# A retention-attention kernel with two feed-forward layers: fewer filler matmuls at the first pair, and two rows of weights converted later in the attention

## The chip, the cores and the metric

The kernel runs on one core of one Trainium2 chip. The metric is device time in microseconds (us), the median of repeated executions. Three executions of the kernel before took 845.58, 846.1 and 847.55 us, so its median is 846.1 us.

## The reference

The program computes a retention attention (no softmax: the scores are multiplied by a decay table), and then two feed-forward layers on its output. Cut to what matters:

```python
scores = q @ k.T / sqrt(64)                  # 4 batches, 8 heads, 576 positions, 64 wide
ret    = (scores * Dmat) @ v                 # Dmat[n, m] = gamma_h ** (n - m) for n >= m, else 0
x  = ret as (2304 tokens, 512)
h  = x @ w_in                                # layer one: 512 -> 2048 -> 512
x  = (max(h, 0) + alpha * min(h, 0)) @ w_out
h  = x @ w2_in                               # layer two, the same sizes
out = (h / (1 + exp(-1.702 * h))) @ w2_out
```

The weights of both layers arrive as 64-bit floats. The kernel turns them into 32-bit floats on the chip, and each of those into two words, high and low, whose three largest cross products stand for one product.

## The kernel before, in words

**Attention.** The 32 heads are worked in 16 pairs. Pair i loads its `ld` (queries, keys, values, 864 KB) and `kts` (keys once more, 256 KB). TensorE computes the scores (`sc`, `a_scores`), then the states (`st`, `a_outer`), and after them the values of the pair before (`av`, `a_values`). VectorE multiplies the scores by the decay (`r`, L305), sums the states (L320, L325, L330) and takes the finished values of the pair before out of PSUM (`xs`, L350). ScalarE scales `kts` and takes the states out. So in pair i VectorE does r(i), the three sums of i, and xs(i-1), in that order, and TensorE's `av` of pair i waits for xs(i-1), which frees its PSUM bank. At pair 0 there is no pair before; `fill(14)` puts 14 matmuls on zeros there (`wps`, L708), and 8 more stand at the very start.

**Weight rows.** Layer one's weights come in 16 rows (128 of the 2048 hidden channels each; 128 x 1024 64-bit numbers in two loads, `raw`). A row is converted by one ScalarE operation (`w_abs`, L116), and on VectorE by two tensor_scalar operations (`w_clamp`, L120 and L123), `w_top` (L130) and `w_low` (L137). Then ScalarE copies the high words (`w_hi`, L85) and VectorE subtracts to get the low words (`w_lo`, L88). `raw` has two slots, so the load of row m waits for `w_low` of row m-2. Between these, `xa_split` cuts finished attention output into high and low words for layer one.

**Order.** Every engine works in program order. The order of the row operations is written as a list of events with due times: `at(t, ...)` puts one in, and `run_to(t)`, called at fixed places of the pair loop (at i, i + 0.25 and i + 0.75), emits all that are due. One unit of time is one pair; layer one starts at `base` = 17 and one unit there is one step. `pace` has the due time of each row, `ahead` how much earlier its load is issued, `d` the distance of its operations.

**Layer one.** A step multiplies one block of tokens by one row: `mm1` (12 matmuls of 512 columns into `h`, L403), then the activation (two ScalarE operations L413, L414 and one VectorE operation L415 into `g`), its split into two words (`gsf`, ScalarE L85 and VectorE L88), and `mm2` (12 matmuls into `acc`, L446), which comes two steps later. So TensorE's order at the start is mm1 of steps 0, 1 and 2 (36 matmuls), mm2 of step 0, mm1 of step 3, and so on. Steps 0, 1 and 2 use rows 0, 1 and 2. The first two matmuls of a step's mm1 need only the high words of its row, the third is the first that needs the low words.

Of the kernel before, what the change touches and what calls it, by code (L numbers as in the profile page):

```python
# [39 lines left out]
def kernel(  # L40
# [52 lines left out]
    def at(time, fn, *args):  # L93
        events.append((time, len(events), fn, args))

    def run_to(time):
        while events and events[0][0] <= time:
            _, _, fn, args = events.pop(0)
            fn(*args)
# [46 lines left out]
    def w_lo(key):  # L146
        sub(nc.vector, wt[key][:, 1], cvs.pop(key).rearrange(both, c=2), wt[key][:, 0])

    def w_words(t, key, src, ahead, d):
        at(t - ahead, w_load, key, src, key[1] % 2)  # L150
        at(t - ahead + (1.0 if ahead > 2 else 0), w_piece, key, src, 1)
        for i, fn in enumerate((w_abs, w_clamp, w_top, w_low)):
            at(t + d * i, fn, key)

    def quarter(j, e, c):
        return cvs[2, 2 * j + e][:, c * 256:c * 256 + 256]
# [80 lines left out]
    def a_load(i):  # L237
        b, p = PAIRS[i]
        t = tmp("ld", i, [128, 1728])
        if i == 0:  # L240
            nc.sync.dma_start(out=t[:, 0:512], in_=qkv[b, p, :, 0:512])
            nc.sync.dma_start(out=mask_sb, in_=mask)
            nc.sync.dma_start(out=vtab_sb, in_=vtab)
            nc.sync.dma_start(out=t[:, 512:1152], in_=qkv[b, p, :, 512:1152])
            nc.sync.dma_start(out=kts[:, 0], in_=kn[b, p])
            nc.sync.dma_start(out=t[:, 1152:1728], in_=qkv[b, p, :, 1152:1728])
        else:
            nc.sync.dma_start(out=t, in_=qkv[b, p])
            nc.sync.dma_start(out=kts[:, i % 4], in_=kn[b, p])
        if i == 1:  # L250
            nc.sync.dma_start(out=otab_sb[:, :, 0:128], in_=otab)
        q = [t[:, j * 128:j * 128 + 128] for j in (0, 1, 4, 5)] + [t[:, 768:832]]
        k = [t[:, j:j + 128] for j in (256, 384, 832, 960)] + [t[:, 1088:1152]]
        ld[i] = q, k, t[:, 1152:1728].rearrange("p (n d) -> p n d", n=9)
# [4 lines left out]
    def a_tables(p):  # L259
        for e in range(2):  # L260
            scale(diag_sb[:, p, e, 0], mask_sb[:, 0:128], vtab_sb[:, p, e:e + 1])
        scale(tail_sb[:, p], mask_sb[:, 128:192], vtab_sb[:, p, 2:3])

    def a_otab(p):
        o = otab_sb[:, p]
        for n in (128, 256):
            copy(o[:, n:2 * n], o[:, 0:n])
        copy(o[:, 512:S], o[:, 0:S - 512])
# [6 lines left out]
    def a_keys(i):  # L275
        n = kts[:, i % 4].rearrange("p (j n) -> p j n", j=4)
        for e, o in enumerate(halves):
            scale(n[:, :, o], n[:, :, o], vtab_sb[:, PAIRS[i][1], e:e + 1])
        k_t[i] = n

    def a_scores(i):
        q, k = ld[i][0:2]
        t = aps.tile([128, 2, 512], F32, tag="sc", name="sc", bufs=2)
        for j in range(4):
            for e, o in enumerate(halves):
                mm(t[:, e, j * 128:j * 128 + 128], k[j][o], q[j][o], j == 0, True)
        sc_t[i] = t

    def a_outer(i):
        q, k, v = ld[i]  # L290
        t = s_t[i] = aps.tile([128, 512], F32, tag="st", name="st")
        for o in halves:
            mm(t[o, 0:64], k[4][o], q[4][o], True, True)
        n = k_t.pop(i)
        for j in range(4):
            for e, o in enumerate(halves):
                mm(t[o, j * 64 + 64:j * 64 + 128], n[:, j, o], v[:, 2 * j + e], False, True)

    def a_evac(i):
        r = tmp("r", i, [128, 1600])  # L300
        r_t[i] = (
            r[:, 0:1024].rearrange("p (e n) -> p e n", e=2), r[:, 1024:1536],
            r[:, 1088:1600].rearrange("p (b n) -> p b n", b=2)[:, :, 0:64],
        )
        nc.vector.tensor_tensor(  # L305
            out=r[:, 0:1024].rearrange("p (e j n) -> p e j n", e=2, j=4),
            in0=sc_t.pop(i).rearrange("p e (j n) -> p e j n", j=4),
            in1=diag_sb[:, PAIRS[i][1]].to_broadcast([128, 2, 4, 128]), op=ALU.mult,
        )


    def a_states(i):
        p = PAIRS[i][1]
        s = r_t[i][1]
        scale(s[:, 0:320], s_t.pop(i)[:, 0:320], vtab_sb[:, p, 3:4])

    def a_sums(i):
        p = PAIRS[i][1]
        s = r_t[i][1]
        nc.vector.scalar_tensor_tensor(  # L320
            out=s[:, 320:512], in0=s[:, 64:256], scalar=vtab_sb[:, p, 3:4], in1=s[:, 128:320],
            op0=ALU.mult, op1=ALU.add,
        )
        half = r_t[i][2]
        nc.vector.scalar_tensor_tensor(  # L325
            out=s[:, 384:512].rearrange("p (b n) -> p b n", b=2), in0=half,
            scalar=vtab_sb[:, p, 4:5], in1=s[:, 384:512].rearrange("p (b n) -> p b n", b=2),
            op0=ALU.mult, op1=ALU.add,
        )
        nc.vector.tensor_tensor(out=s[:, 0:64], in0=s[:, 0:64], in1=tail_sb[:, p], op=ALU.mult)  # L330

    def a_values(i):
        q, _, v = ld[i]
        r, s = r_t.pop(i)[0:2]
        t = av_t[i] = aps.tile([128, 1024], F32, tag="av", name="av")
        out = [t[:, A0 + j * 128:A0 + j * 128 + 128] for j in range(4)] + [t[:, A0 + 512:A0 + S]]
        for c in range(1, 5):
            s0 = 64 if c == 1 else 192 + c * 64
            for o in halves:
                mm(out[c][o], s[o, s0:s0 + 64], q[c][o], c < 3, False)  # L340
        for o in halves:
            mm(out[4][o], v[o, 8], s[o, 0:64], False, True)
        for j in range(4):
            for e, o in enumerate(halves):
                mm(out[j][o], v[:, 2 * j + e], r[:, e, j * 128:j * 128 + 128], False, True)

    def a_out(i):
        if i % 3 == 0:
            xs_t[i // 3] = tmp("xs", i // 3, [128, 3, S])
        nc.vector.tensor_tensor(  # L350
            out=xs_t[i // 3][:, i % 3], in0=av_t.pop(i)[:, A0:A0 + S], in1=otab_sb[:, PAIRS[i][1]],
            op=ALU.mult,
        )
        ld.pop(i)
# [326 lines left out]
    wz = att.tile([128, 128], F32, name="wz")  # L681
    n_a = len(PAIRS)
    base = n_a + 1
    pace = [3.6, 8.6, 14.1]
    pace += [base + t for t in (0.8, 2.35, 3.9, 5.45, 7.0, 8.8, 10.6, 12.4, 14.2, 15.9, 17.6, 19.3, 21.4)]
    ahead = {0: 2.6, 1: 3.2, 2: 3.2}
    for m, t in enumerate(pace):
        d = 0.75 if m < 3 else 0.5
        w_words(t, (1, m), w1, ahead.get(m, 1.6), d)
        at(t + 3 * d + 0.25, w_hi, (1, m))  # L690
        at(t + 4 * d + 0.25, w_lo, (1, m))
    for i in range(n_a):
        b = PAIRS[i][0]
        for c in range(2):
# [6 lines left out]
    with tc.manual_schedule():  # L701
# [4 lines left out]
        def fill(n):  # L706
            for i in range(n):
                nc.tensor.matmul(out=wps[:, 0, 0:128], lhsT=wz, rhs=wz, start=True, stop=True)  # L708
# [5 lines left out]
        for i in range(n_a + 1):  # L714
            if i < n_a:
                a_scores(i)
                if i < NP:
                    a_tables(i)
                a_keys(i)
                a_evac(i)  # L720
            run_to(i)
            if i < n_a:
                a_outer(i)
                a_states(i)
                a_sums(i)
            run_to(i + 0.25)
            if i:
                if i <= NP:
                    a_otab(i - 1)
                a_values(i - 1)  # L730
                a_out(i - 1)
            else:
                fill(14)
            if i + 3 < n_a:
                a_load(i + 3)
            run_to(i + 0.75)
# [14 lines left out]
        for n, (_, c, m0, _) in enumerate(BLOCKS[N_FIRST:], 1):  # L751
            homes[c] = xp[n % 2]
            for k in range(NK):
                t = starts[c, m0] - (4 if n == 1 else 4.4) + 0.9 * k
# [160 lines left out]
```

## Time and profile before

| | |
|---|---|
| median of three executions | 846.1 us |
| the profiled execution | 845.46 us, its span 843.7 us, mean granted TensorE clock 0.993 |
| TensorE matmuls | busy 826.7 us, 98% of the span |
| TensorE weight loads | 753.0 us, 89% |
| VectorE | 633.7 us, 75% |
| ScalarE | 458.5 us, 54% |
| attention, from the first instruction to layer one's first matmul | 80.27 us |

The profile is one execution, in microseconds from its first instruction. A row of the timeline gives the start, the time until the last of its merged instructions ended, the engine (PE is TensorE, PEld its weight loads, DVE VectorE, ACT ScalarE), the source line, the operation with out<-in, and in brackets how long the engine had stood idle before it and what ended that. On TensorE one 32-bit matmul of the attention is recorded as two.

### The profile page before, as it was taken

The numbers are of one execution on the slowest core, as the hardware profiler recorded it, in microseconds if no ns is written. First come the engines' busy times: TensorE is split into PE (matmuls) and PEld (weight loads), VectorE is DVE, ScalarE is ACT, GpSimd is POOL, SyncE is SP. The second block draws the span as 40 slices with busy tenths as digits, with TensorE's granted clock in tenths as the row PEclk, the third lists the DMA queues.
The fourth block names the chain that finished last, engine by engine and source line by source line (L and its number), as shares of the span: only waits on it lengthen the run. The fifth ranks groups of instructions, "written<-read, shape, count | busy, mean of one in ns | idle before, by whom it ended". The sixth has DMA issues, their size and how long they took to land.

```text
span 843.7 us, 13989 instructions
## 1 busy us (share of the span) xinstructions
PE 826.7 (98%) x5132; PEld 753.0 (89%) x5132; DVE 633.7 (75%) x1128; ACT 458.5 (54%) x920; POOL 17.7 (2%) x36
## 2 busy tenths in 40 slices
PE   9999999999999998899999999999999999999998
PEld 8788888888888886698888899999999999999998
DVE  3997887687483776666768697789787699677875
ACT  5643664554353445445534676666566576566553
POOL 0000000000000010000010000000000000000000
PEclk9999999999999999999999999999999999999999
DMA  8985843455065465646656544598543877545872
GB/s 309 318 302 171 271 154 104 151 188 175 18 234 204 115 201 172 204 154 205 194 151 219 198 157 132 197 325 303 179 130 109 319 265 269 172 130 177 293 271 78
DMA packets 66100, 166.97 MB, mean 198 GB/s; under 512 B 7152, under 2 KB 33392, under 8 KB 60272
## 3 DMA queue, kind: packets, MB, share of 16 engines
q1 hardware_dynamic: 61424, 149.30, 51.8%
q0 software_dynamic: 4608, 16.78, 6.8%
q8 instruction: 40, 0.66, 0.3%
q14 instruction: 28, 0.23, 0.1%
HBM read 128.83 MB, written 37.22 MB: 197 GB/s over the span
## 4 chain that ended last, share of the span: by engine, by line
PE 55%; DMA 3%; DVE 2%; issue 1%; ACT 1%; SPq 0%; DVEq 0%; ACTq 0%
PE acc L567 23%; PE h L567 18%; PE acc L446 7%; PE h L403 6%; DMA rg<-sums 2%; DMA sg<-cv 1%; DMA sg<-sums 0%; DVE gsf L88 0%; ACT gsf L85 0%; DVE cv L130 0%; DVE sums L200 0%; DVE cv L120 0%; DVE g L415 0%; SPq L211 0%; DVE sums L474 0%
## 5 line engine op out<-in xcount | busy, mean ns | idle before, releaser
L446 PE MATMUL acc<-gsf,w 128*128 128x512 f32 (+1 forms) x960 | 214.6, 373 | 8.2 <-ACT gsf L85 7.1
L403 PE MATMUL h<-x,w 128*128 128x512 f32 (+1 forms) x960 | 212.2, 370 | 0.0
L446 PEld LDWEIGHTS acc<-gsf,w 128*128 128x128 f32 x960 | 170.3, 191 | 40.9 <-ACT gsf L85 8.1
L403 PEld LDWEIGHTS h<-x,w 128*128 128x128 f32 x960 | 169.8, 191 | 31.1 <-DVE w L88 0.8
L85 ACT ACTIVATE gsf<-g 128x384 fp32r<-128x384 f32 (+2 forms) x248 | 132.8, 543 | 104.3 <-DVE g L415 62.7
L88 DVE TENSOR_TENSOR gsf<-g,gsf 128x384 fp32r<-128x384 f32 (+2 forms) x248 | 141.6, 580 | 54.9 <-ACT gsf L85 54.4
L415 DVE SCALAR_TENSOR_TENSOR g<-h,nalpha_sb,g 128x512 f32<-128x512 f32 (+1 forms) x80 | 55.6, 695 | 77.0 <-ACT h L414 76.8
L567 PE MATMUL acc<-x,ws 128*128 128x384 f32 x552 | 106.8, 334 | 0.0
L567 PE MATMUL acc<-gsf,ws 128*128 128x384 f32 x576 | 101.3, 334 | 0.0
L567 PEld LDWEIGHTS acc<-gsf,ws 128*128 128x128 f32 x576 | 100.0, 188 | 0.0
L567 PEld LDWEIGHTS acc<-x,ws 128*128 128x128 f32 x552 | 96.7, 188 | 0.0
L567 PE MATMUL h<-x,ws 128*128 128x384 f32 x456 | 90.3, 334 | 0.0
L413 ACT ACTIVATE g<-h 128x512 f32<-128x512 f32 (+1 forms) x80 | 43.9, 549 | 73.3 <-PE h L403 73.3
L567 PEld LDWEIGHTS h<-x,ws 128*128 128x128 f32 x456 | 80.1, 188 | 0.1
L567 PE MATMUL h<-gsf,ws 128*128 128x384 f32 x432 | 76.6, 334 | 0.0
L567 PEld LDWEIGHTS h<-gsf,ws 128*128 128x128 f32 x432 | 75.0, 188 | 0.2 <-DVE gsf L88 0.2
L474 DVE TENSOR_TENSOR tm<-h,tm 128x384 f32<-128x384 f32 x73 | 40.5, 555 | 32.0 <-PE h L567 27.8
L88 DVE TENSOR_TENSOR ws<-rw,ws 128x512 fp32r<-128x512 f32 x96 | 57.0, 617 | 0.0
L474 DVE TENSOR_TENSOR g<-g,g 128x384 f32<-128x384 f32 x93 | 51.5, 554 | 0.7
L85 ACT ACTIVATE ws<-rw 128x512 fp32r<-128x512 f32 x96 | 49.8, 569 | 0.2 <-DMA rw<-rg 0.2
L414 ACT ACTIVATE h<-h 128x512 f32<-128x512 f32 (+1 forms) x80 | 43.9, 549 | 0.0
L116 ACT ACTIVATE cv<-raw 128x1024 f32<-128x1024 f32 x32 | 36.3, 1133 | 6.6 <-DMA raw<-in_w_dram 5.0
(73 smaller groups left out, 702.5 us busy)
## 6 DMA issues: line engine op xcount, KB each, us to landing
ws<-sg SPq DMA_DIRECT2D x42, 1024.0 KB, 6.2
raw<-in_w_dram SPq DMA_DIRECT2D x32, 512.0 KB, 4.9
raw<-in_w_dram POOLq DMA_DIRECT2D x32, 512.0 KB, 5.0
ld<-in_qkv_dram SPq DMA_DIRECT2D x15, 864.0 KB, 6.1
rw<-rg SPq DMA_DIRECT2D x24, 512.0 KB, 3.5
rw<-rg SPq DMA_DIRECT2D x24, 384.0 KB, 3.1
sg<-sums SPq DMA_DIRECT2D x40, 128.0 KB, 2.1
kts<-in_kn_dram SPq DMA_DIRECT2D x16, 256.0 KB, 6.3
```

Of the source, the lines that this page charges most:

```text
L85: return nc.scalar.activation(out=out, in_=in_, func=ACTF.Copy)
L88: return eng.tensor_tensor(out=out, in0=a, in1=b.bitcast(F32), op=ALU.subtract)
L116: nc.scalar.activation(out=cvs[key], in_=raws[key][:, :, 1].bitcast(F32), func=ACTF.Abs)
L403: nc.tensor.matmul(out=t, lhsT=w[:, cw, k * 128:k * 128 + 128], rhs=x[:, cx], start=(i == 0), stop=(i == 3 * NK - 1),)
L413: nc.scalar.activation(out=g, in_=t, func=ACTF.Relu)
L414: nc.scalar.activation(out=t, in_=t, func=ACTF.Relu, scale=-1.0)
L415: nc.vector.scalar_tensor_tensor(out=g, in0=t, scalar=nalpha_sb[:, m:m + 1], in1=g, op0=ALU.mult, op1=ALU.add)
L446: nc.tensor.matmul(out=acc[0][d], lhsT=w[:, cw, d * 128:d * 128 + 128], rhs=g[:, cx], start=(m == m0 and i == 0), stop=(m == m1 - 1 and i ...
L474: nc.vector.tensor_tensor(out=out, in0=x, in1=y, op=op)
L567: nc.tensor.matmul(out=out, lhsT=w(cw), rhs=x(cx), start=(start and n == 0), stop=True, skip_group_check=True,)
```

## The change

Three things change. Pair 0 gets 5 filler matmuls for 14. Rows 0 and 1 are due at 8.0 and 12.0 (they were at 3.6 and 8.6), and their VectorE operations are put one pair apart, each at the end of a pair, behind xs. Row 2 is due at 16.1 (it was at 14.1), so that its VectorE operations begin after the last xs and end within layer one's first steps. The due times of rows 3 to 6 move by 0.05 to 0.3, and `w_lo` of rows 0 and 1 is due a little earlier relative to `w_hi`.

```diff
-    def w_words(t, key, src, ahead, d):
+    def w_words(t, key, src, ahead, d, first):
         at(t - ahead, w_load, key, src, key[1] % 2)
         at(t - ahead + (1.0 if ahead > 2 else 0), w_piece, key, src, 1)
-        for i, fn in enumerate((w_abs, w_clamp, w_top, w_low)):
-            at(t + d * i, fn, key)
+        at(t, w_abs, key)
+        for i, fn in enumerate((w_clamp, w_top, w_low)):
+            at(t + first + d * i, fn, key)
...
-    pace = [3.6, 8.6, 14.1]
-    pace += [base + t for t in (0.8, 2.35, 3.9, 5.45, 7.0, ...)]
-    ahead = {0: 2.6, 1: 3.2, 2: 3.2}
+    pace = [8.0, 12.0, 16.1]
+    pace += [base + t for t in (1.1, 2.55, 4.0, 5.5, 7.0, ...)]
+    ahead = {0: 6.0, 1: 6.0, 2: 3.2}
     for m, t in enumerate(pace):
-        d = 0.75 if m < 3 else 0.5
-        w_words(t, (1, m), w1, ahead.get(m, 1.6), d)
+        d = 0.5 if m > 1 else 1.0
+        w_words(t, (1, m), w1, ahead.get(m, 1.6), d, 0.75 if m < 2 else d)
         at(t + 3 * d + 0.25, w_hi, (1, m))
-        at(t + 4 * d + 0.25, w_lo, (1, m))
+        at(t + 4 * d - (0.25 if m < 2 else -0.25), w_lo, (1, m))
...
-                fill(14)
+                fill(5)
```

One line was added near the top, so a line of the changed kernel below L149 has a number that is greater by one.

**VectorE in the attention.** First the kernel before, from r(6) on, where row 0 is converted (cv_383 and raw_212 are row 0; xs_438 takes values out, x_461 and x_505 are the split of attention output):

```order
L305 TENSOR_TENSOR r_459<-sc_448,diag_sb_80 128x1024
L88 TENSOR_TENSOR x_461<-xs_438,x_461 128x512
L320 SCALAR_TENSOR_TENSOR r_459<-r_459,vtab_sb_78 128x192
L325 SCALAR_TENSOR_TENSOR r_459<-r_459,vtab_sb_78 128x128
L330 TENSOR_TENSOR r_459<-r_459,tail_sb_81 128x64
L130 SCALAR_TENSOR_TENSOR cv_383<-raw_212,cv_383 128x1024
L350 TENSOR_TENSOR xs_438<-av_480,otab_sb_82 128x576
L88 TENSOR_TENSOR x_505<-xs_438,x_505 128x64
L305 TENSOR_TENSOR r_519<-sc_508,diag_sb_80 128x1024
L137 SCALAR_TENSOR_TENSOR cv_383<-raw_212,cv_383 128x1024
L320 SCALAR_TENSOR_TENSOR r_519<-r_519,vtab_sb_78 128x192
```

Now the changed kernel from r(10) on, where its row 0 is converted (cv_615, raw_261, w_794):

```order
L306 TENSOR_TENSOR r_724<-sc_713,diag_sb_80 128x1024
L321 SCALAR_TENSOR_TENSOR r_724<-r_724,vtab_sb_78 128x192
L326 SCALAR_TENSOR_TENSOR r_724<-r_724,vtab_sb_78 128x128
L331 TENSOR_TENSOR r_724<-r_724,tail_sb_81 128x64
L351 TENSOR_TENSOR xs_760<-av_741,otab_sb_82 128x576
L137 SCALAR_TENSOR_TENSOR cv_615<-raw_261,cv_615 128x1024
L306 TENSOR_TENSOR r_777<-sc_766,diag_sb_80 128x1024
L321 SCALAR_TENSOR_TENSOR r_777<-r_777,vtab_sb_78 128x192
L326 SCALAR_TENSOR_TENSOR r_777<-r_777,vtab_sb_78 128x128
L331 TENSOR_TENSOR r_777<-r_777,tail_sb_81 128x64
L351 TENSOR_TENSOR xs_760<-av_796,otab_sb_82 128x576
L88 TENSOR_TENSOR w_794<-cv_615,w_794 128x1024
```

Before, `w_top` stands between the sums and xs and `w_low` between r and the sums, with splits of attention output in the same pairs; now each pair has one conversion operation, behind xs.

**VectorE where layer one begins.** The kernel before, from the last xs on (cv_969, raw_797 and w_1067 are row 2; g_1092 and g_1119 are the activations of steps 0 and 1, gsf the split of one):

```order
L350 TENSOR_TENSOR xs_1064<-av_1045,otab_sb_82 128x576
L137 SCALAR_TENSOR_TENSOR cv_969<-raw_797,cv_969 128x1024
L737 TENSOR_SCALAR nalpha_sb_84<-alpha_sb_83 128x16
L415 SCALAR_TENSOR_TENSOR g_1092<-h_1079,nalpha_sb_84,g_1092 128x512
L88 TENSOR_TENSOR w_1067<-cv_969,w_1067 128x1024
L88 TENSOR_TENSOR gsf_1078<-g_1092,gsf_1078 128x512
L415 SCALAR_TENSOR_TENSOR g_1119<-h_1099,nalpha_sb_84,g_1119 128x512
```

The changed kernel, from the last xs on (row 2 is cv_1028, raw_888 and w_1101; the steps are g_1079 and g_1107):

```order
L351 TENSOR_TENSOR xs_1049<-av_1030,otab_sb_82 128x576
L120 TENSOR_SCALAR cv_1028<-cv_1028 128x1024
L123 TENSOR_SCALAR cv_1028<-cv_1028 128x1024
L738 TENSOR_SCALAR nalpha_sb_84<-alpha_sb_83 128x16
L416 SCALAR_TENSOR_TENSOR g_1079<-h_1066,nalpha_sb_84,g_1079 128x512
L130 SCALAR_TENSOR_TENSOR cv_1028<-raw_888,cv_1028 128x1024
L88 TENSOR_TENSOR gsf_1065<-g_1079,gsf_1065 128x512
L137 SCALAR_TENSOR_TENSOR cv_1028<-raw_888,cv_1028 128x1024
L416 SCALAR_TENSOR_TENSOR g_1107<-h_1086,nalpha_sb_84,g_1107 128x512
L88 TENSOR_TENSOR w_1101<-cv_1028,w_1101 128x1024
```

Before, `w_low` of row 2 comes directly behind the last xs, and `w_lo` (w_1067) ahead of step 1's activation. Now all five VectorE operations of row 2 come behind the last xs; `w_top` and `w_low` stand behind step 0's activation, and `w_lo` (w_1101) behind step 1's.

**ScalarE at the same place.** Before (w_1067 is `w_hi` of row 2):

```order
L85 ACTIVATE w_1067<-cv_969 128x1024
L413 ACTIVATE g_1092<-h_1079 128x512
L414 ACTIVATE h_1079<-h_1079 128x512
L85 ACTIVATE gsf_1078<-g_1092 128x512
L116 ACTIVATE cv_1115<-raw_1042 128x1024
L413 ACTIVATE g_1119<-h_1099 128x512
L414 ACTIVATE h_1099<-h_1099 128x512
```

And changed (w_1101 is `w_hi` of row 2):

```order
L116 ACTIVATE cv_1028<-raw_888 128x1024
L414 ACTIVATE g_1079<-h_1066 128x512
L415 ACTIVATE h_1066<-h_1066 128x512
L85 ACTIVATE gsf_1065<-g_1079 128x512
L85 ACTIVATE w_1101<-cv_1028 128x1024
L414 ACTIVATE g_1107<-h_1086 128x512
L415 ACTIVATE h_1086<-h_1086 128x512
L116 ACTIVATE cv_1111<-raw_1051 128x1024
```

`w_hi` of row 2 was ahead of the activation of step 0; now it stands between the two ScalarE operations of step 0 and those of step 1, and it waits for `w_low`.

## Rows read from the trace of the kernel before

**Rows 1.** PE timeline at pair 0's fillers: start, us, engine, line, out<-in, count.
```profile
10.73 2.17 PE L708 MATMUL wps<-wz 128*128 128x128 f32 x18
12.84 0.38 PE L271 MATMUL sc<-ld 64*128 64x128 f32 x2
```
**Rows 2.** DMA issues at 3.55 us: size, us from issue to landing.
```profile
ld<-in_qkv_dram SPq DMA_DIRECT2D x1, 864.0 KB, 6.9
```
**Rows 3.** ACT timeline: kts of pair 1.
```profile
11.11 0.91 ACT L257 ACTIVATE kts<-kts,vtab_sb 128x256 f32<-128x256 f32 x2 [0.61 <-DMA kts<-in_kn_dram]
```
**Rows 4.** PE timeline: scores of pairs 13 and 15, the last values, layer one.
```profile
64.73 1.16 PE L271 MATMUL sc<-ld 64*128 64x128 f32 x16
...
72.78 1.16 PE L271 MATMUL sc<-ld 64*128 64x128 f32 x16
...
74.75 0.99 PE L271 MATMUL av<-ld,r 64*64 64x128 f32 x16
...
78.21 0.99 PE L271 MATMUL av<-ld,r 64*64 64x128 f32 x16 [1.33 <-DVE xs L350]
...
80.27 2.12 PE L403 MATMUL h<-x,w 128*128 128x512 f32 x8
```
**Rows 5.** Waits up to 140 us: us in total, times, longest.
```profile
PE av L271 <- DVE xs L350: 2.6, 3, 1.3
...
PE st L271 <- ACT kts L257: 1.1, 2, 0.9
```
**Rows 6.** DVE timeline: row 1's operations among pairs 10 and 11; pair 14's xs.
```profile
52.13 0.68 DVE L120 TENSOR_SCALAR cv<-cv 128x1024 f32<-128x1024 f32 x1
...
53.45 0.62 DVE L88 TENSOR_TENSOR x<-xs,x 128x448 fp32r<-128x448 f32 x1
53.99 1.22 DVE L305 TENSOR_TENSOR r<-sc,diag_sb 128x1024 f32<-128x1024 f32 x1
55.12 0.41 DVE L320 SCALAR_TENSOR_TENSOR r<-r,vtab_sb 128x192 f32<-128x192 f32 x1
...
55.84 0.22 DVE L330 TENSOR_TENSOR r<-r,tail_sb 128x64 f32<-128x64 f32 x1
55.97 1.22 DVE L130 SCALAR_TENSOR_TENSOR cv<-raw,cv 128x1024 int32<-128x1024 int32 x1
57.10 0.75 DVE L350 TENSOR_TENSOR xs<-av,otab_sb 128x576 f32<-128x576 f32 x1
57.77 1.22 DVE L305 TENSOR_TENSOR r<-sc,diag_sb 128x1024 f32<-128x1024 f32 x1
...
72.90 0.76 DVE L350 TENSOR_TENSOR xs<-av,otab_sb 128x576 f32<-128x576 f32 x1 [0.51 <-PE av L271]
```
**Rows 7.** Timeline of all engines at layer one's start.
```profile
82.31 1.06 ACT L85 ACTIVATE w<-cv 128x1024 fp32r<-128x1024 f32 x1 [6.87 <-DVE cv L137]
...
84.47 0.75 DVE L415 SCALAR_TENSOR_TENSOR g<-h,nalpha_sb,g 128x512 f32<-128x512 f32 x1 [2.10 <-ACT h L414]
85.13 1.22 DVE L88 TENSOR_TENSOR w<-cv,w 128x1024 fp32r<-128x1024 f32 x1
...
86.40 2.17 PEld L403 LDWEIGHTS h<-x,w 128*128 128x128 f32 x10 [0.35 <-DVE w L88]
86.83 0.58 ACT L413 ACTIVATE g<-h 128x512 f32<-128x512 f32 x1
...
87.92 0.75 DVE L415 SCALAR_TENSOR_TENSOR g<-h,nalpha_sb,g 128x512 f32<-128x512 f32 x1 [0.97 <-ACT h L414]
...
88.84 2.89 PE L446 MATMUL acc<-gsf,w 128*128 128x512 f32 x12
```
**Rows 8.** PE timeline: two long waits later in layer one.
```profile
325.83 4.58 PE L446 MATMUL acc<-gsf,w 128*128 128x512 f32 x12 [2.61 <-ACT gsf L85]
...
346.82 4.87 PE L446 MATMUL acc<-gsf,w 128*128 128x512 f32 x12 [3.65 <-ACT gsf L85]
```
**Rows 9.** Busy time by stretch: us, PE, PEld, DVE, ACT, POOL (x), PEclk, DMA, GB/s.
```profile
348.00:349.00 1.00, 1.00 (x4) 0.78 (x3) 0.48 (x2) 0.65 (x2) 0.00 (x0) 0.50 0.20 74
```

More of the change, by code (lines that the diff above doesn't have):

```diff
@@ L683 @@
     base = n_a + 1
-    pace = [3.6, 8.6, 14.1]
-    pace += [base + t for t in (0.8, 2.35, 3.9, 5.45, 7.0, 8.8, 10.6, 12.4, 14.2, 15.9, 17.6, 19.3, 21.4)]
-    ahead = {0: 2.6, 1: 3.2, 2: 3.2}
+    pace = [8.0, 12.0, 16.1]
+    pace += [base + t for t in (1.1, 2.55, 4.0, 5.5, 7.0, 8.8, 10.6, 12.4, 14.2, 15.9, 17.6, 19.3, 21.4)]
+    ahead = {0: 6.0, 1: 6.0, 2: 3.2}
     for m, t in enumerate(pace):
-        d = 0.75 if m < 3 else 0.5
-        w_words(t, (1, m), w1, ahead.get(m, 1.6), d)
+        d = 0.5 if m > 1 else 1.0
+        w_words(t, (1, m), w1, ahead.get(m, 1.6), d, 0.75 if m < 2 else d)
         at(t + 3 * d + 0.25, w_hi, (1, m))
-        at(t + 4 * d + 0.25, w_lo, (1, m))
+        at(t + 4 * d - (0.25 if m < 2 else -0.25), w_lo, (1, m))
     for i in range(n_a):
```

## The prediction

> **What bounds the kernel now.** I read the busy times first: TensorE is busy for 98% of the span (the table above), so an edit counts only by the TensorE time that it takes away or adds. Then I listed busy times by stretches of 5 us for the attention, and TensorE's timeline, because the change touches only the first 90 us. Three things are to be seen there.
>
> First, after pair 0's fillers the attention runs at a fixed pace where nothing is in its way: from pair 13 to pair 15 the scores start 8.05 us apart, so a pair is 4.025 us of TensorE [rows 4]. Pair 1 starts at 12.84 [rows 1] and pair 15 at 72.78, that is 59.94 us for 14 pairs, and 14 x 4.025 = 56.35. So 3.59 us are lost in between, in waits for VectorE's xs and for ScalarE's kts, and in the slower start behind them [rows 5]. They lie in the pairs where a row is converted.
>
> Second, the last values start 5.43 us behind the last scores (78.21 - 72.78) because two conversion operations stand ahead of the xs that they wait for [rows 4]; layer one starts 2.06 us after that, at 80.27.
>
> Third, layer one's step 2 is the first that needs row 2. Its low words come at 85.13 + 1.22 = 86.35, TensorE goes on at 86.40 after a wait of 0.35, and reaches mm2 of step 0 at 88.84 [rows 7]. From there on TensorE waits for nothing before the late waits of 2.61 and 3.65 us in layer one [rows 8]; the chain there comes out of activations, so it moves with TensorE.
>
> **The fillers.** The last 18 of the 28 records, nine fillers, run from 10.73 to 12.84 [rows 1]. Without them pair 1 could start at 10.73. Its `ld` lands at 3.55 + 6.9 = 10.45 [rows 2], in time; its kts is scaled by 11.11 + 0.91 = 12.02 [rows 3], and the states begin some 1.36 us behind the scores, at 12.1. That fits with nothing to spare. Gain: 2.11 us. Bounds: 1.2, if the landing sets the start in an execution where the fillers ran faster, and 2.2.
>
> **Rows 0 and 1.** One conversion operation per pair now stands behind xs. By the start-to-start times VectorE needs for a pair: r 1.13, the first two sums 0.72, the third 0.13, xs 0.67, which is 2.65 us; top, low and `w_lo` take 1.13 each, the two clamps together 1.32, and a split of 448 columns 0.54 [rows 6]. Pairs 10 to 15 then come to 3.78 (3.97 with the clamps), under 4.025. Pairs 8 and 9 still have a split: 4.51 and 4.32, together 0.78 us too much. That is hidden: xs ends at 72.90 + 0.76 = 73.66 and is needed at 74.75, a spare of 1.1 us, and later pairs catch up [rows 4, 6]. `w_hi` stands a pair behind `w_low`, so ScalarE no longer waits with kts queued behind it. The load pieces of row 0 move past the loads of one more pair in SP's queue, but each still stands behind a pair's `ld` and kts, as one did before at an undisturbed pace; I count them at nothing, and up to 1 us if two pieces in neighbouring pairs make a kts late. So the 3.59 us go. At the end the last xs but one starts at the undisturbed place, about 4.14 us behind the scores, and the last values 5.04 us behind them, which saves 0.39 us. Gain: 3.98 us, bounds 3.0 and 4.0. Layer one's first matmul then comes at 80.27 - 2.11 - 3.98 = 74.18.
>
> **Row 2.** This part costs. All five of its VectorE operations come behind the last xs, in the order clamps, activation of step 0, top, split of step 0, low, activation of step 1, `w_lo`, while ScalarE has `w_hi` between the two activations. I count from layer one's first matmul (T), with durations of [rows 7]. The activation of step 0 on VectorE begins at 84.47 - 80.27 = T + 4.20, as now, since it waits for mm1. The clamps end long before that. Top begins 0.66 later, at 4.86; the split at 5.99 (its ScalarE half is done by then); a split of 512 columns delays the next by some 0.60 (0.54 for 448 [rows 6], scaled), so low begins at 6.59 and ends at 7.81. `w_hi` waits for it, and runs from 7.84 to 8.90. Step 1's ScalarE operations are queued behind `w_hi` and begin 0.97 after its start, at 8.81; its VectorE operation comes 1.09 later (86.83 to 87.92), at 9.90; `w_lo` begins at 10.57 and ends at 11.79; TensorE gets the third matmul of step 2 at T + 11.84. Before, this was 86.40 - 80.27 = T + 6.13. So TensorE has nothing to do between the end of step 1 (T + 5.4) and `w_hi`, does two matmuls, and waits again. Cost: 5.7 us, bounds 5.4 and 6.1. Nothing else can fill it, as steps 0 to 2 of mm1 stand ahead of every mm2 on TensorE.
>
> Behind the wait, VectorE has the split and activation of steps 0 and 1 already done, and SP issues row 4's load at `w_low` of row 2, at T + 7.85, so as many us ahead of `w_lo`'s end as before. Low of row 4 falls behind the copies out of `acc`; I laid the operations out to step 9, and the rows come 0.5 us or more before TensorE wants them. I count 0, with 0.5 as the upper bound.
>
> **The clock.** Long waits cost twice. After the waits of 2.61 and 3.65 us the 12 matmuls behind them took 4.58 and 4.87 us [rows 8], where 12 take 2.89 [rows 7], so 1.7 and 2.0 us more, and the granted clock in such a stretch was 0.50, the 1.2 GHz level [rows 9]. The wait of 1.33 at the end of the attention [rows 4] did no such thing. The new wait, 3.5 and 2.4 us with two matmuls between, is of the long kind. I take 1.8, near both rows. Bounds: 0, if it falls only inside the wait itself, and 3.7, two such falls.
>
> **Sum.** -2.11 - 3.98 + 5.7 + 1.8 = +1.4 us on the profiled execution's 845.46, which is 846.9. The median of the three runs lies 0.64 above that execution, so I forecast 847.5 us, 0.17% above the median of before. A difference under 0.2% (1.7 us) is about what a measurement can't tell from none.
>
> **A rule against the change.** The start-to-start times above are shorter than the durations: L130 begins at 55.97 and lasts 1.22, but the next operation begins at 57.10, 0.09 before its end, and L320 (0.41) holds two operations within 0.72 [rows 6]. The Trainium skill (VectorE: DVE Perf Modes, "The DRAIN you can't avoid") says that the next VectorE operation does not start until the pipe of the one before has emptied, which would let no operation begin inside another. By durations (r 1.22, sums 0.41 + 0.35 + 0.22, xs 0.75) pairs 8 to 15 would hold 34.9 us of VectorE work against 32.2 of TensorE, and by the start-to-start times 31.7. The trace does not agree with the rule as I read it here, so the sum goes by the start-to-start times; the rule's outcome is the fourth rival.
>
> **Rivals.**
> 1. The clock falls for two spells, not one: the second part of the wait (2.4 us) holds it at 1.2 GHz for as long again after step 2 resumes. For it: that part alone is about as long as the 2.61 us that was enough once. Against it: part of the first spell passes while TensorE is idle anyway. Cost 3.6 for 1.8, time 849.3, slower. It decides from the point where the granted clock is still 0.50 four us after step 2 goes on.
> 2. The clock costs nothing. For it: the two matmuls inside the wait. Against it: both rows of long waits. Time 845.7, no change.
> 3. The wait for row 2 is much shorter, because something in the chain low, `w_hi`, activation, `w_lo` runs beside and not behind. For it: nothing but that the chain is long. Against it: each of its links is one engine's program order. If 3 us of it went, and with them most of the clock's cost, the time would be 843, faster.
> 4. The attention keeps a wait: VectorE's queue in pairs 8 to 15 does not fit, or a kts is late. 34.9 - 32.2 = 2.7 us too much, less the spare of 1.1, leaves 1.6: time 849.1, slower. Against it: the rows' spacing.
> 5. The late waits of layer one are set by transfers and not by TensorE, and take up the clock's part: 846, no change.
>
> **Chances and range.** Forecast 0.58 (own range 846.2 to 848.8, and somewhat more of it below 847.8 than above); rival 1 0.15; rival 2 0.08; rival 3 0.07; rival 4 0.07; rival 5 0.05. Within 0.2% (844.4 to 847.8): 0.36 of the forecast, 0.08 and 0.05, so 0.49. Slower: 0.22 + 0.15 + 0.07, so 0.44. Faster: 0.07. The range that leaves out no more than 2 in 10 takes in rivals 1, 2, 4 and 5: 845.1 to 849.7.
>
> **What would show it.** Right: pair 1's scores near 10.7; scores 4.03 us apart from pair 2 to 15; layer one's first matmul near 74.2; on TensorE a wait of some 3.5 us for `w_hi` and one of some 2.4 us for `w_lo` near 86; a granted clock of 0.50 just behind it; mm2 of step 0 near 90.1. Wrong: a layer one that begins after 75.5; a single short wait at step 2; a clock that stays at 1.00 there; or a new wait of TensorE between 90 and 130 us.

## The result: slower, by three times what was forecast

The changed kernel takes 851.19 us (median of 6 runs, 849.79 to 852.41) against 846.67 for the kernel before (6 runs): a ratio of 1.0053, 95% interval 1.0036 to 1.0070, so 3.0 to 5.9 us slower. The forecast was 847.5. The profiled execution of the changed kernel took 852.41 us, 6.95 more than that of the kernel before (845.46). I split it at two places that every trace shows: T, layer one's first matmul, and the first mm2 (step 0). Before: 80.27, then 8.57, then 756.62 to the end. After: 75.92, then 16.19, then 760.30. The differences are -4.35, +7.62 and +3.68.

The attention first: TensorE's timeline of the changed kernel, scores of pairs 1, 9 and 15, the last values, and layer one's start (answering to [rows 1, 4, 7]).
```profile
11.18 1.16 PE L272 MATMUL sc<-ld 64*128 64x128 f32 x16 [1.45 <-DMA ld<-in_qkv_dram]
...
44.25 1.16 PE L272 MATMUL sc<-ld 64*128 64x128 f32 x16 [0.51 <-DMA ld<-in_qkv_dram]
...
68.81 1.16 PE L272 MATMUL sc<-ld 64*128 64x128 f32 x16
...
73.86 0.99 PE L272 MATMUL av<-ld,r 64*64 64x128 f32 x16 [0.95 <-DVE xs L351]
...
75.92 5.78 PE L404 MATMUL h<-x,w 128*128 128x512 f32 x24
84.89 1.03 PE L404 MATMUL h<-x,w 128*128 128x512 f32 x2 [3.20 <-ACT w L85]
87.79 4.48 PE L404 MATMUL h<-x,w 128*128 128x512 f32 x10 [1.86 <-DVE w L88]
92.11 2.89 PE L447 MATMUL acc<-gsf,w 128*128 128x512 f32 x12
```
Pair 1 starts 1.66 us earlier, not 2.11, because its load has not landed at 10.73. The waits for xs in the middle are gone; the last values start 5.05 us behind the last scores, as worked out (5.04). But pair 9 waits for its load, and from pair 1 to layer one it takes 64.74 us, against 67.43 before and 63.45 in the forecast. Then come the two waits for row 2: high words, two matmuls, low words. The third matmul of step 2 stands at 87.79 - 75.92 = T + 11.87 (forecast 11.84), and mm2 of step 0 4.32 us later, where it was 2.44 later before [rows 7].

Why row 2 is late is seen on VectorE, same kernel (start, us, engine, line, operation).
```profile
80.13 0.75 DVE L416 SCALAR_TENSOR_TENSOR g<-h,nalpha_sb,g 128x512 f32<-128x512 f32 x1 [1.93 <-ACT h L415]
80.80 1.22 DVE L130 SCALAR_TENSOR_TENSOR cv<-raw,cv 128x1024 int32<-128x1024 int32 x1
81.93 0.69 DVE L88 TENSOR_TENSOR gsf<-g,gsf 128x512 fp32r<-128x512 f32 x1
82.53 1.22 DVE L137 SCALAR_TENSOR_TENSOR cv<-raw,cv 128x1024 int32<-128x1024 int32 x1
85.85 0.75 DVE L416 SCALAR_TENSOR_TENSOR g<-h,nalpha_sb,g 128x512 f32<-128x512 f32 x1 [2.10 <-ACT h L415]
86.52 1.22 DVE L88 TENSOR_TENSOR w<-cv,w 128x1024 fp32r<-128x1024 f32 x1
```
It is the order of the forecast: activation, top, split, low, (high words on ScalarE), activation, low words; only the hand-overs to ScalarE and back leave gaps. Behind it the clock is low (columns: busy us of PE, PEld, DVE, ACT, POOL, granted clock, DMA share, GB/s; answers to [rows 9]).
```profile
85.00:90.00 5.00, 3.14 (x7) 2.03 (x8) 3.78 (x5) 2.37 (x4) 0.00 (x0) 0.51 0.93 306
90.00:95.00 5.00, 5.00 (x19) 4.03 (x18) 1.51 (x2) 1.82 (x4) 0.00 (x0) 0.80 0.46 177
```

The part that I had put at nothing: TensorE's timeline of the changed kernel at steps 9 and 10.
```profile
127.47 3.07 PE L404 MATMUL h<-x,w 128*128 128x512 f32 x12
130.38 2.89 PE L447 MATMUL acc<-gsf,w 128*128 128x512 f32 x12
133.10 0.61 PE L404 MATMUL h<-x,w 128*128 128x512 f32 x2
135.87 4.14 PE L404 MATMUL h<-x,w 128*128 128x512 f32 x10 [2.15 <-DVE w L88]
139.85 2.92 PE L447 MATMUL acc<-gsf,w 128*128 128x512 f32 x12
```
At 130.38 the changed kernel is 3.46 us behind the kernel before (126.92 there); at 139.85 it is 7.19 behind (132.66). Step 10 waits for the low words of row 7, and the ten matmuls behind the wait take 3.98 us. ScalarE and VectorE of the same kernel show what they stand behind.
```profile
130.85 1.06 ACT L85 ACTIVATE w<-cv 128x1024 fp32r<-128x1024 f32 x1 [0.50 <-DVE cv L137]
131.82 1.10 ACT L116 ACTIVATE cv<-raw 128x1024 f32<-128x1024 f32 x1
132.82 0.59 ACT L414 ACTIVATE g<-h 128x512 f32<-128x512 f32 x1
```
```profile
106.60 1.29 DVE L468 COPY os<-acc 128x512 f32<-128x512 f32 x2
107.80 1.22 DVE L137 SCALAR_TENSOR_TENSOR cv<-raw,cv 128x1024 int32<-128x1024 int32 x1
...
129.60 1.22 DVE L137 SCALAR_TENSOR_TENSOR cv<-raw,cv 128x1024 int32<-128x1024 int32 x1
...
133.93 0.75 DVE L416 SCALAR_TENSOR_TENSOR g<-h,nalpha_sb,g 128x512 f32<-128x512 f32 x1 [2.51 <-ACT h L415]
134.60 1.22 DVE L88 TENSOR_TENSOR w<-cv,w 128x1024 fp32r<-128x1024 f32 x1
```
ScalarE has row 7's high words and row 8's abs ahead of step 9's activation, VectorE has row 7's low words behind that activation. This order is that of the kernel before. In the kernel before, though, low of row 7 ran at 123.61, 5.99 us earlier, while TensorE was only 3.46 us earlier. The delay goes back to row 4: its low, at 107.80, stands behind the two copies out of `acc`. In the kernel before it stands ahead of them. Its VectorE timeline:
```profile
99.20 1.22 DVE L137 SCALAR_TENSOR_TENSOR cv<-raw,cv 128x1024 int32<-128x1024 int32 x1
...
103.12 1.29 DVE L467 COPY os<-acc 128x512 f32<-128x512 f32 x2
```
Low of row 4 frees the buffer for raw row 6, so SP issues that load at 100.48 before and at 109.08 after. SP's timelines, before and then after:
```profile
100.48 0.82 SPq L112 DMA_DIRECT2D raw<-in_w_dram  x2
```
```profile
109.08 0.81 SPq L112 DMA_DIRECT2D raw<-in_w_dram  x2
```
From row 6 it goes on to row 7 through two engines. In the changed kernel ScalarE's abs of row 6 waits 4.18 us for that load (in the kernel before it waits for none). The ScalarE half of a split is queued behind this abs, and VectorE waits 2.04 us for it. From then on VectorE has no gap left in which to catch up: it is busy for 13.88 of the 14.10 us from 117.40 to 131.50. ScalarE and VectorE, changed kernel:
```profile
115.79 1.13 ACT L116 ACTIVATE cv<-raw 128x1024 f32<-128x1024 f32 x1 [4.18 <-DMA raw<-in_w_dram]
```
```profile
117.47 0.69 DVE L88 TENSOR_TENSOR gsf<-g,gsf 128x512 fp32r<-128x512 f32 x1 [2.04 <-ACT gsf L85]
```
Row 7 had nothing to spare in the kernel before either. VectorE and TensorE there:
```profile
128.97 1.22 DVE L88 TENSOR_TENSOR w<-cv,w 128x1024 fp32r<-128x1024 f32 x1
```
```profile
129.64 3.18 PE L403 MATMUL h<-x,w 128*128 128x512 f32 x12
```
Its low words end at 130.19, the third matmul of step 10 could have started at 130.09 (two matmuls behind 129.64), and the step takes 3.02 us to the next start where the others take 2.72.

### The profile page after: what moved, and what is told of

Same layout as the page of the kernel before. It is cut to its first block, busy times and chain, and to the rows that moved or that the text cites. A ratio compares the mean times of both kernels' runs of the same rounds, so it can differ in the third digit from the quotient of the medians.

```text
span 850.6 us, 13949 instructions
## 1 busy us (share of the span) xinstructions
PE 827.8 (97%) x5114; PEld 752.6 (88%) x5114; DVE 634.0 (75%) x1128; ACT 458.1 (54%) x920; POOL 17.7 (2%) x36
## 4 chain that ended last, share of the span: by engine, by line
PE 84%; DVE 6%; DMA 5%; issue 2%; ACT 2%; SPq 1%; DVEq 0%; ACTq 0%
PE acc L568 23%; PE h L404 18%; PE h L568 18%; PE acc L447 18%; PE av L272 3%; DMA rg<-sums 3%; DMA ld<-in_qkv_dram 2%; PE sc L272 2%; PE st L272 1%; DVE cv L137 1%; DVE g L416 1%; DVE cv L130 1%; DVE gsf L88 1%; DVE w L88 1%; DMA sg<-sums 1%
## 5 line engine op out<-in xcount | busy, mean ns | idle before, releaser
L404 PE MATMUL h<-x,w 128*128 128x512 f32 (+1 forms) x960 | 216.5, 376 | 7.2 <-DVE w L88 4.0
L404 PEld LDWEIGHTS h<-x,w 128*128 128x128 f32 x960 | 172.0, 193 | 40.1 <-DVE w L88 5.4
```

The costliest lines, as they stand in the source:

```text
L404: nc.tensor.matmul(out=t, lhsT=w[:, cw, k * 128:k * 128 + 128], rhs=x[:, cx], start=(i == 0), stop=(i == 3 * NK - 1),)
```

## The experiments

Times as a ratio to the kernel before, run beside it, with the 95% interval; 0.001 is 0.85 us. T, mm2 of step 0 behind T, and the rest are of the one profiled execution.

| kernel | ratio | T | to mm2 | rest |
|---|---|---|---|---|
| changed | 1.0053 (1.0036 to 1.0070) | 75.92 | 16.19 | 760.30 |
| a1_fill14 | 1.0075 (1.0055 to 1.0095) | 76.78 | 16.02 | 760.67 |
| a2_row2_front | 1.0016 (1.0002 to 1.0031) | 74.16 | 9.54 | 762.42 |
| a3_lo7_front | 1.0028 (1.0016 to 1.0041) | 74.48 | 16.26 | 757.68 |
| a4_fill_wait | 1.0036 (1.0021 to 1.0051) | 74.27 | 14.23 | 760.57 |
| b1_pace | 1.0046 (1.0029 to 1.0063) | 75.32 | 17.60 | 756.97 |
| b3_before_fill5 | 0.9980 (0.9965 to 0.9994) | 81.39 | 8.57 | 756.47 |
| b2_combo | 0.9948 (0.9934 to 0.9962) | 76.91 | 8.30 | 758.56 |
| b2_combo3 | 0.9949 (0.9933 to 0.9965) | 75.99 | 8.30 | 756.92 |
| c1_row2_as_before | 0.9956 (0.9944 to 0.9968) | 76.36 | 8.96 | 755.93 |
| c2_spaced | 0.9946 (0.9931 to 0.9961) | 74.09 | 8.29 | 757.97 |

**The clock (a4).** Fillers in the first part of the wait.
```diff
+            if i == 2:
+                t = mps.tile([128, 512], F32, tag="acc3", name="idle")
+                for _ in range(22):
+                    nc.tensor.matmul(out=t, lhsT=wt[1, 0][:, 0, 0, 0:128], rhs=x_t[0, 0, 0][:, 0], ...)
```


> The changed kernel with 22 matmuls of 128x512 that compute nothing, put on TensorE between mm1 of step 1 and mm1 of step 2, where it waits for row 2's high words: so TensorE works through the first part of the wait and no chain changes. Theory: the ten matmuls behind the wait take 4.32 us in place of 2.44 because the clock fell during it. Then with the gap filled the granted clock at 85 to 95 us is higher (0.51 and 0.80 in the changed kernel), the third to twelfth matmul take 2.4 to 3.2 us, and mm2 of step 0 comes 1.1 to 1.9 us earlier than 16.19 us behind layer one's first matmul; the total falls by 0 to 1.9 us, as row 7's low words behind VectorE's queue can take it back at step 10. Rival: the ten matmuls are slow for another cause (operands that arrive, PSUM that is read meanwhile); then they take 4.3 us as before, or the fillers come to stand in the way and mm2 of step 0 is later.

TensorE's timeline, and the stretch of the wait:
```profile
79.84 5.15 PE L793 MATMUL idle<-x,w 128*128 128x512 f32 x22
...
86.10 2.56 PE L404 MATMUL h<-x,w 128*128 128x512 f32 x10 [0.65 <-DVE w L88]
88.50 2.88 PE L447 MATMUL acc<-gsf,w 128*128 128x512 f32 x12
```
```profile
85.00:90.00 5.00, 4.35 (x19) 3.27 (x19) 3.07 (x5) 1.78 (x4) 0.00 (x0) 1.00 1.03 383
```
Row 2 is no earlier (86.10 - 74.27 = T + 11.83), but the clock stays at 1.00 and the ten matmuls take 2.40 us, not 4.32. So 1.9 us of the loss at step 2 were the clock's (the two traces differ by 1.96). Step 10's wait is as before, and didn't take it back. The ratio fell by 0.0017, 1.4 us, with intervals that overlap, so the times alone don't show it; the trace does.

**Row 2's place (a2).**
```diff
+        if m == 2:
+            ...
+            for n, fn in enumerate((w_abs, w_clamp, w_top, w_low, w_hi, w_lo)):
+                at((t, 16.6, 16.65, 16.7, 16.72, 16.74)[n], fn, (1, m))
+            continue
```


> The changed kernel with all five VectorE operations of row 2 (clamps, top, low, low words) directly behind the last xs, ahead of the activation of step 0. Theory: the wait for row 2 is what the queue ahead of the low words makes it (layer one's first matmul + 11.87 for the third matmul of step 2), and the slow clock comes of that wait. Then the third matmul comes 6.5 to 7.3 us behind layer one's first one, the granted clock at 85 to 95 us stays near 1.00, mm2 of step 0 comes some 7 us earlier than at + 16.19, and the time is 5 to 7.6 us under the changed kernel's, as far as step 10's later wait for row 7 doesn't take it back: VectorE and the loads ahead of step 10 move with TensorE by the same theory, so that wait stays near 2 us. Rival: the late rows (row 7) come when they come, whatever TensorE does before; then the wait at step 10 grows by what is gained here, and the time stays within 1 us of the changed kernel's.

```profile
81.29 2.57 PE L404 MATMUL h<-x,w 128*128 128x512 f32 x10 [0.53 <-DVE w L88]
83.70 2.88 PE L447 MATMUL acc<-gsf,w 128*128 128x512 f32 x12
...
129.54 2.56 PE L404 MATMUL h<-x,w 128*128 128x512 f32 x10 [2.19 <-DVE w L88]
131.94 2.88 PE L447 MATMUL acc<-gsf,w 128*128 128x512 f32 x12
```
The third matmul comes at T + 7.13 and mm2 of step 0 6.65 us earlier than in the changed kernel: the wait was VectorE's queue. But the ratio fell by 0.0037 only, 3.1 us, where I had expected 5 to 7.6, and the rest is 2.1 us longer than in the changed kernel. Of that, 0.5 us are there by mm2 of step 8 (at 131.94, and at 139.85 in the changed kernel): VectorE's copies out of `acc`, now late, cost a wait of 1.08, row 6's low words one of 0.62, and row 7's still 2.19, this time at the full clock. The other 1.6 us come later, 1.2 of them after 346 us, and the runs don't show why. So neither theory held in full. Step 10's wait stayed near 2 us, as the first had it, and didn't grow, as the rival had it, so it doesn't come of the late row 2; but waits that neither had came up beside it.

**Row 7's place (a3).**
```diff
-        at(t + 4 * d - (0.25 if m < 2 else -0.25), w_lo, (1, m))
+        at(t + 4 * d - (0.25 if m < 2 else -0.25) - (0.3 if m == 7 else 0), w_lo, (1, m))
```


> The changed kernel with the low words of row 7 put one place earlier on VectorE, ahead of the activation of step 9. Theory: the 2.15 us that TensorE waits at step 10, and the slow clock behind it, come from that one place in VectorE's order (activation of step 9 ends at 134.60, low words at 135.82). Then step 10's third matmul comes 0.7 to 1.9 us earlier, its wait falls under 1.5 us, the clock at 135 to 140 us stays near 1.00 (0.66 in the changed kernel), and the time is 2 to 3.7 us under the changed kernel's. Rival: row 7 is late because its raw words land late and VectorE is busy without a gap before them; then the low words only change places with an activation that TensorE needs next, the wait is as long one step on, and the time stays within 1 us of the changed kernel's.

```profile
132.29 2.88 PE L404 MATMUL h<-x,w 128*128 128x512 f32 x12
135.01 2.88 PE L447 MATMUL acc<-gsf,w 128*128 128x512 f32 x12
```
This is step 10: it runs through without a wait (2.72 us to the next start). The rest is 2.62 us shorter, and the ratio falls by 0.0025, 2.1 us. The theory's size in the trace is met, at its lower end.

**Rows 3 to 6 (b1).**
```diff
-    pace += [base + t for t in (1.1, 2.55, 4.0, 5.5, 7.0, ...)]
+    pace += [base + t for t in (0.8, 2.35, 3.9, 5.45, 7.0, ...)]
```


> The changed kernel with the due times of rows 3 to 6 set back to those of the kernel before (0.8, 2.35, 3.9, 5.45 in place of 1.1, 2.55, 4.0, 5.5); rows 0 to 2 and row 7 as changed. By this the low step of row 4 stands again ahead of the two copies out of acc, so SP gets the load of raw row 6 some 2 to 5 us earlier. Theory: step 10's wait for row 7 comes of these small shifts of rows 3 to 6, which make raw rows 6 and 7 land late, and not of row 7's own place. Then that wait falls from 2.15 to under 0.7 us and the time is 2 to 3.7 us under the changed kernel's (a ratio to before of 1.001 to 1.003), with step 2's wait as in the changed kernel (third matmul at layer one's first + 11.9). Rival: the wait comes of VectorE's backlog that the late row 2 leaves, or of row 7's place alone; then step 10 still waits about 2 us and the ratio stays near 1.005.

```profile
88.49 4.63 PE L404 MATMUL h<-x,w 128*128 128x512 f32 x10 [3.00 <-DVE w L88]
```
Step 10 has no wait any more, and the rest falls by 3.33 us to 756.97, that of the kernel before (756.62): these four due times are the cause of the late row 7. No run moves one of the four alone. But the traces of all runs agree with the path by row 4 and row 6's load: where low of row 4 stands behind the copies out of `acc` (the changed kernel, a1 to a4), VectorE waits 1.78 to 2.04 us for a split behind row 6's abs, and where it stands ahead of them (the kernel before, b1 to b3, c1, c2), it does not. But the clamps of row 3 now stand ahead of row 2's low words; the third matmul comes at T + 13.17, 1.30 later, and the trace keeps 1.9 of the 3.3 us. In the times 0.0007 is left, 0.6 us, which can't be told from nothing. I had expected step 2 to stay as it was: wrong.

**The fillers (a1, b3).** Each changes one number, `fill(5)` to `fill(14)` in the changed kernel, and the reverse in the kernel before.

> The changed kernel with 14 filler matmuls at the first pair in place of 5, all else as changed. The step on record: nine fillers are worth 2.11 us, so this is 2.1 us slower than the changed kernel, pair 1's scores near 12.9 and layer one's first matmul near 78.0 (75.92 in the changed kernel). Rival: in the changed kernel pair 1 already waits for its load, and its scores start at 11.18; then the fillers give back 12.84 - 11.18 = 1.66 at most, and where later pairs wait for loads that land when they land, the lateness at pair 9 and at pairs 10 to 15 shrinks by what pair 1 starts later: layer one then begins between 75.9 and 77.6, and the time is 0 to 1.7 us above the changed kernel's.

> The kernel before with 5 fillers in place of 14, nothing else. Theory on record: nine fillers are worth up to 2.11 us, bounded by the landing of pair 1's load: pair 1's scores start at 10.6 to 11.2 (12.84 before), and 1.6 to 2.1 us of it reach the end: ratio 0.9975 to 0.998. Rival: the attention of before waits for xs and for kts where two operations of a row stand in one pair, and for loads that land when they land; then part of it is taken up there and the ratio is 0.998 to 1.000, with layer one's first matmul between 79 and 80.3.

The changed kernel loses 0.0022 (1.9 us, intervals overlap, so not told from nothing), the kernel before gains 0.0020 (0.5 to 3.0 us on 846.85). Both agree with 2.11 less what the landing holds back; pair 1's scores start at 10.58 in b3. In a1 they start at 11.59, only 0.41 later than in the changed kernel, since the 14 fillers ran from 8.27 to 11.59 there and from 9.04 to 12.84 in the kernel before; layer one begins 0.86 later, in the rival's range and not near the 78.0 of the step on record. b3's profiled execution nevertheless begins layer one 1.1 us later than the kernel before, since at pair 4 a kts stands behind the abs of a row whose load landed late, and the clock falls (ScalarE, TensorE, and a stretch):
```profile
24.03 1.15 ACT L116 ACTIVATE cv<-raw 128x1024 f32<-128x1024 f32 x1 [1.66 <-DMA raw<-in_w_dram]
25.07 0.90 ACT L257 ACTIVATE kts<-kts,vtab_sb 128x256 f32<-128x256 f32 x2
```
```profile
25.63 1.07 PE L271 MATMUL st<-ld,kts 128*64 128x64 f32 x16 [1.37 <-ACT kts L257]
```
```profile
27.50:30.00 2.50, 2.50 (x28) 2.05 (x24) 0.71 (x3) 1.50 (x5) 0.00 (x0) 0.50 0.18 61
```
From pair 4's scores, at 22.84, to pair 5's it takes 7.03 us there.

**Without the third part (c1).** Fillers and rows 0 and 1 as changed, rows 2 to 6 as before.
```diff
-    pace = [8.0, 12.0, 16.1]
+    pace = [8.0, 12.0, 14.1]
...
+        if m == 2:
+            ...
+                at(t + (0, 0.75, 1.5, 2.25, 2.5, 3.25)[n], fn, (1, m))
```


> The changed kernel without its third part: 5 fillers and the new due times of rows 0 and 1, but row 2 (load, abs, clamps, top, low, high and low words) and rows 3 to 6 at the due times of the kernel before. So pairs 14 and 15 hold two conversion operations each. Theory: the loss sits in the third part, and the first two parts keep most of their gain; VectorE then has 5.10 and 4.91 us of work in pairs 14 and 15 against 2 x 4.025, 2.0 us too much, of which the spare of some 1.1 us hides a half: layer one's first matmul at 74.9 to 76.2, the third matmul of step 2 some 6.1 us behind it and mm2 of step 0 some 8.6, the clock at 1.00, no wait at step 10: 4 to 5.4 us faster than before, ratio 0.9935 to 0.9955. Rival: row 2 had to leave the attention for the others to fit; then the backlog runs into the last xs and the last values: layer one begins after 77 and the ratio is 0.997 or more.

```profile
73.20 1.11 PE L272 MATMUL av<-ld,r 64*64 64x128 f32 x16 [2.04 <-DVE xs L351]
74.05 2.38 PE L272 MATMUL av<-r,ld 64*64 64x64 f32 x20
76.36 9.13 PE L404 MATMUL h<-x,w 128*128 128x512 f32 x36
```
The first two parts by themselves are 0.0044 faster than before (4.0 us of its median there, 845.4), and the third part costs 0.0097, 8.2 us. VectorE's backlog is there (the last values wait 2.04 us, 1.09 more than after, and the next 20 matmuls take 2.38 us for 1.34), and is worth 2.2 us: from pair 1 to T it takes 65.81 us, where a2 to a4 took 63.6. I had expected a T of 74.9 to 76.2 and a clock at 1.00; T is 76.36, and the granted clock was 0.53 from 75 to 77.5 us.

**A better version (b2_combo, b2_combo3, c2).** Row 2's clamps go into VectorE's gap ahead of the last xs, the rest of it directly behind that xs, and rows 3 to 6 get their old due times.
```diff
+        if m == 2:
+            at(12.0, w_load, (1, m), w1, 0)
+            at(12.0 + 1.0, w_piece, (1, m), w1, 1)
+            for n, fn in enumerate((w_abs, w_clamp, w_top, w_low, w_hi, w_lo)):
+                at((15.3, 15.8, 16.6, 16.65, 16.7, 16.74)[n], fn, (1, m))
+            continue
```


> The changed kernel with three things put right: row 2's load and abs earlier, its clamps behind the low words of row 1 (in VectorE's gap ahead of the last xs) and its top, low and low words directly behind the last xs; and the due times of rows 3 to 6 of the kernel before. Theory: the whole loss is the place of row 2 and of rows 3 to 6, and the first two parts of the change keep their gain. Then layer one begins at 74.1 to 75, the third matmul of step 2 comes 5.6 to 6.2 us behind it, mm2 of step 0 8.2 to 8.8 us behind it, and no wait over 0.7 us follows up to 160 us: 5.5 to 6.6 us faster than before, a ratio of 0.992 to 0.994. Rival: step 10's wait (2.2 us, and up to 1.3 us of clock) stays, as it did with row 2 alone in front: ratio 0.995 to 0.997. Second rival: the clamps ahead of the last xs delay the end of the attention by more than the 0.1 us that they stand over: layer one begins after 75.5.

> As b2_combo, and the low words of row 7 also ahead of the activation of step 9 on VectorE, as in a3_lo7_front. Theory: if the place of rows 3 to 6 is the whole cause of step 10's wait, this changes nothing against b2_combo (within 0.3 us in the same chip's runs, a ratio of 0.992 to 0.994). Rival: row 7's own place still costs a wait in b2_combo, and then this one is 1 to 3.5 us faster than b2_combo.

> As b2_combo3, with the two load pieces of rows 0 and 1 two pairs apart (behind pairs 3, 5, 7 and 9) in place of behind neighbouring pairs (2 and 3, 6 and 7). Theory: where the attention of the changed kernel is slower than 4.025 us a pair from pair 2 on, it is that two pieces in neighbouring pairs make the loads of a later pair late; layer one's first matmul then comes 63.5 to 63.8 us behind pair 1's scores (64.74 in the changed kernel, 64.56 in b2_combo3), and the time is 0 to 1 us under b2_combo3's. Rival: the lateness is that of the execution, whatever the place of the pieces (63.6 in three of the other runs with the pieces in neighbouring pairs); then the two don't differ in their times.

c2_spaced at layer one's start:
```profile
74.09 8.46 PE L404 MATMUL h<-x,w 128*128 128x512 f32 x36
```
Steps 0 to 2, 36 matmuls, run through without a wait, and mm2 of step 0 follows at T + 8.3 in all three. All three are 0.0051 to 0.0054 faster than before. That is less than I expected (0.006 to 0.008): b2_combo began layer one at 76.91, since pair 1 started at 12.32 (why stands below) and its scores took 2.08 us for 1.16; the clamps ahead of the last xs, the second rival, are not the cause, as c2 has them too and takes 63.65 us from pair 1 to T. All three keep a wait that I hadn't expected, of 0.61 to 0.83 us for VectorE's copies out of `acc` (0.83 at 102.52 in b2_combo). A wait of 0.60 for row 7's low words is left in b2_combo and none in b2_combo3, with no difference in time. Where the load pieces stand makes none either: 63.65 us from pair 1 to T in c2, but also 63.58 to 63.64 in a2, a3 and a4, which have the pieces where the changed kernel has them.

## Why the prediction was wrong

**What bounds the kernel, and the fillers.** Right. The gain of 2.11 is bounded by pair 1's load, as written, and in the changed kernel's execution it decides: 1.66. In ten profiled executions with 5 fillers pair 1 starts at 10.44 to 12.32, so 2.4 to 0.5 us ahead of 12.84. Where it starts latest, in b2_combo, it is not that load: pair 0's own loads were late (its scores waited 1.09 us for `ld`, 0.41 in the kernel before, and its states 0.91 for kts), and the fillers behind ran at the 1.2 GHz level (granted clock 0.50 from 9 to 12 us). The last ten filler records in the changed kernel, and in b2_combo:
```profile
8.35 1.38 PE L709 MATMUL wps<-wz 128*128 128x128 f32 x10
```
```profile
9.88 2.50 PE L715 MATMUL wps<-wz 128*128 128x128 f32 x10
```
That I hadn't thought of.

**Rows 0 and 1.** Right in mechanism and nearly in size. T was forecast at 74.18, and 75.92 is behind 75.5, one of the marks that I had set for being wrong. Five executions have the changed kernel's instructions up to the last pair: T at 74.16, 74.27, 74.48, 75.32 and 75.92. The last is the one shown above, with 0.45 us from pair 1's load and 1.3 from later lateness: from pair 1 to T it gained 67.43 - 64.74 = 2.69 us, just under my bound of 3.0, where a2 to a4 gained 3.8. Why loads land at other times in other executions, the runs don't show. VectorE's queue did fit, by the start-to-start times: the only wait for xs is the one at the end. The fourth rival, which followed from the Trainium skill's rule on emptying the pipe (VectorE: DVE Perf Modes, "The DRAIN you can't avoid"), did not occur; the trace of the changed kernel agrees with that reading as little as that of the kernel before. The same section of the Trainium skill adds that a next operation that isn't held starts earlier, and sends its reader on to "Two Vector instructions with no wait between them"; the trace agrees with that (a start 1.13 us behind that of a 1.22 us operation).

**Row 2 and the clock.** Right in both. T + 11.87 for 11.84; 1.88 us of clock for 1.8, and a4 shows that it was the clock. The size differs between executions: in a3 the ten matmuls took 4.43 us and the 12 of mm2 behind them 3.47, 2.8 us more than in a4 and between the 1.8 of the forecast and the 3.6 of rival 1. In the changed kernel's execution rivals 1 to 3 fall: the wait is there, it cost clock, and mm2 of step 0, at T + 16.19 (8.57 + 5.7 + 1.8 = 16.1), already takes 2.89 us for its 12 matmuls, as at the full clock. The fifth falls too: the late waits of layer one, 2.22 and 3.70 us at 332.67 and 353.71 (2.61 and 3.65 before [rows 8]), took up 0.3 us: the changed kernel is 7.19 us behind at 139.85 and 6.89 at the second of them. (By its own sum the prediction should have put mm2 of step 0 near 90.25, not 90.1.)

**The step that failed** is "I laid the operations out to step 9, and the rows come 0.5 us or more before TensorE wants them. I count 0, with 0.5 as the upper bound." It measured 3.7 us: a wait of 2.3 us (the third matmul of step 10 at 135.87, where 133.55 was possible), 1.7 of clock behind it, less 0.3 that step 10 loses in the kernel before too. The layout ended one step before the row that is short. Nor is it so that TensorE waits for nothing in the kernel before, as the prediction reads its trace: those 0.3 us at step 10 are the sign that row 7 had nothing to spare. I had seen its beginning, low of row 4 behind the copies out of `acc`, and not followed it to the load of raw row 6 that waits for this low, though that is the same link that I did follow for row 4's own load. b1 shows the cause (old due times, no wait at step 10), and a3 that one place earlier in VectorE's order is enough. With step 10's wait gone, a3 stands at 1.0028 (1.0016 to 1.0041), and the forecast, which had no such wait, at 1.0017. And the mark that I set, a new wait between 90 and 130 us, stopped 4 us short of it.

Forecast and 3.7 us give 846.9 + 3.7 = 850.6 for the profiled execution, and +5.1 between the two kernels, inside the measured 3.0 to 5.9. The 1.7 us by which the attention's profiled execution fell short aren't needed for that, and may be of that execution; no run settles it. The range (845.1 to 849.7) ended too low because the bound of this one term was taken from a layout that didn't contain it.

## What to carry to other kernels

A due time that moves an operation past another changes not only who waits for that operation but which buffer it frees, and so when a load two rows later is issued: follow it until the slack of the row it feeds is known, and give the part beyond your layout a bound from the longest wait seen, with its clock. And price a part of a change by itself: here two parts gained 4 us and the third lost 8, and the third could be had almost free by putting row 2's clamps into a gap of 1.2 us that VectorE had ahead of the last xs and giving rows 3 to 6 their old due times.

## What the runs showed of the hardware

The same wait costs one price or two. Step 10 waited 2.15 us in the changed kernel, 2.20 in a4 and 2.17 in a1, and the ten matmuls behind took 3.98 us each time, at a granted clock of 0.66 from 135 to 140 us in the changed kernel; in a2 it waited 2.19, and they took 2.40, at a granted clock of 1.00:
```profile
130.00:135.00 5.00, 5.00 (x24) 4.12 (x23) 4.20 (x6) 1.72 (x3) 0.00 (x0) 1.00 0.01 2
```
In c1 a wait of 2.04 brought the low clock, and in b3 one of 1.37; in the kernel before one of 1.33 did not (granted clock 1.00 from 75 to 85 us). Why the same wait costs differently, the runs don't show. So a wait of about 2 us is best given both prices, 2 and 3.7 us.
